# Batch 0's hidden layer by seven products, its quarter sums kept in SBUF, and the mean of w1 by one accumulation

## The chip, the cores and the metric

The kernel runs on one core of one Trainium2 chip. It is judged by the device time of one execution, in microseconds (us). Five runs of the kernel before gave a median of 1111.34 us (1110.28 to 1115.63). Changes under about 0.3% (3.3 us) can hardly be told from no change.

The core has five engines, each with its own queue, which works in order: TensorE (PE, matmuls), VectorE (DVE), ScalarE (ACT), GpSimd (POOL) and SyncE (SP, which only issues transfers here). POOL issues transfers too. A transfer is put on a queue behind what that queue holds, and a wait at the head of a queue holds up all that is behind it.

## The reference

Batch 4, 8 heads, 768 rows, 64 columns to a head, all in float32:

1. Hashed attention: six signs of `q @ proj` and of `k @ proj` give each row a bucket; scores count only where the buckets are equal; softmax, times v. The heads side by side give x, 768 x 512 for each batch.
2. `u = x + real(fft2(x))`.
3. `un = (u - mean) / sqrt(var + 1e-6)` along the 512 columns.
4. `out = u + relu(un @ w1) @ w2`, with w1 of 512 x 2048 and w2 of 2048 x 512. The weights come as float64, and the kernel makes float32 of them on the chip.

## The kernel before, in words

Batch b's attention is interleaved, step by step, with the mixing and the two layers of batch b-1: `attention(b)` and `mix(b)` are generators, and the loop at the end of `_main` calls them in turn. A step of attention (`weigh`, `values`) is one block of 128 keys of a pair of heads: scores on PE (L869), exp on ACT (L873), the bucket mask on DVE (L879), the sum of weights `acc` on DVE (L957), the product with v on PE (L890). A pair has six such steps; a batch has four pairs. `scale` sums `acc` over keys on PE (L910) and divides.

The order on PE, DVE, ACT and POOL is set by hand for batch 0's attention (`tc.manual_schedule`), and by the framework's list scheduler after that. Tiles with one tag share a fixed number of buffers. `pt` gives PSUM banks from a ring of two (four more in the last batch and at the very start).

**w1.** `weights1` runs beside batch 0's attention. It converts 16 slices of 128 x 512 (`narrow`, L631 to L647), and takes the mean over the 512 rows out of each column (`centre`, L670). The mean comes from `average`: four matmuls with a 128 x 32 matrix of ones put the sums of the four row chunks side by side on 32 PSUM partitions each (L656, tile `ws`), ACT copies that to SBUF (L661), and one full matmul with `mean`, filled with 1/(32 * 512), adds them up (L664, tile `wm`). The two parts are a step apart. The columns 0 to 1023 are centred during batch 0's attention; for the other 1024 the means are kept and taken off in batch 1's attention (the list `means`).

**w2.** `weights2` converts 16 slices of w2 through a ring of three raw buffers, `zraw2`. POOL issues the load of slice i+3 (L685) after slice i is converted. One conversion is three ACT instructions (L639, which waits for the load, L646 after DVE's L635, L647), and four on DVE (L631, L635, L644 twice); every second one is followed by four DVE sums (L1198 to L1201). The first eight run in `after` beside `mix(0)`'s first steps, the others in the second half of `mlp0`. Each half of w2's quarters is stored to DRAM by seven transfers on SP (L1203).

**The first layer.** w1 has 16 column blocks of 128. Batch 0 uses `mlp0`: each block and each half of the rows (384) takes four matmuls of 128 x 384 into one bank (L1314, tile `h`), and one ACT relu empties it (L1318). That is 128 matmuls of this kind. The batches 1 to 3 use `mlp7`: blocks f and f + 8 together take seven products of quarters (two matmuls each, L1361, tile `h_p`), with sums before and after, as in the Strassen-Winograd scheme: 112 matmuls for a batch. The sums after are seven ACT copies or relus out of PSUM, three relus in SBUF, and five DVE additions for each f. The sums of w1's quarters are made in batch 0: `quarters(f)`, called from the second row blocks of `mlp0`, computes four sums on DVE (L1149 to L1152) into the tile `tq` and stores them, with three plain quarters, in the DRAM tile `ad` (L1154, L1155). `mlp7` loads them from there through a ring of 12, whose place is w1 itself.

**The second layer.** `outer7` uses seven products for all batches (L1232, tile `o`); it uses `tq` for its temporaries too.

**Shared buffers.** `acc` and the four tiles `ef` of `fold` share the tag `t6`, with two buffers. `fold` is DVE work that starts the Fourier step; two of its four steps run in the last pair of the same batch's attention.

Of the kernel before, what the change touches and what calls it, by code (L numbers as in the profile page):

```python
# [479 lines left out]
def _main(  # L480
# [128 lines left out]
    mean = const.tile([P, P], F32, tag="mean", name="mean")  # L609
    nc.gpsimd.memset(mean, 1.0 / (32 * DM))  # L610
    w1 = const.tile([P, NDC, DFF], F32, tag="w1", name="w1")
# [39 lines left out]
    def average(f):  # L651


        ps = pt([P, WC], f"ws{f}")
        for c in range(NDC):
            nc.tensor.matmul(  # L656
                ps[32 * c : 32 * c + 32, :], ones[:, 0:32], w1[:, c, f : f + WC],
                start=True, stop=True,
            )
        part = wt([P, WC], F32, "u", f"part{f}", 2)  # L660
        nc.scalar.copy(part, ps)  # L661
        yield
        ps = pt([P, WC], f"wm{f}")
        nc.tensor.matmul(ps, mean, part, start=True, stop=True)  # L664
        yield ps

# [36 lines left out]
    def weights1():  # L703
        slices = [
            (w1[:, c, f : f + WC], moe_w_ch1[c * P : (c + 1) * P, f : f + WC])
            for f in range(0, DFF, WC)
            for c in range(NDC)
        ]
        zt = wt([P, 3, 2 * WC], F32, "z", "zraw1", 1)
        ft = wt([P, 12, WC], F32, "F", "fraw", 1)  # L710
        raws = [zt[:, i] for i in range(3)] + [
            ft[:, i : i + 2].rearrange("p i w -> p (i w)") for i in range(0, 8, 2)
        ]
        arrival = Arrival(slices, raws, 0)
        for i in range(arrival.depth):
            arrival.fetch(i, nc.sync)
            if i == 1:
                load(1)
        yield
        half = None  # L720
        for i in range(len(slices)):
            arrival.convert(i, ft[:, 8 + i % 4].bitcast(I32))
            yield
            if half:
                centre(half[0], next(half[1]))
                half = None
            if i % NDC == NDC - 1:


                f = i // NDC * WC  # L730
                if f < DFF // 2:
                    half = f, average(f)
                    next(half[1])

# [190 lines left out]
    def attention(b):  # L925
# [10 lines left out]
        for t in range(NPAIR):  # L936
            n = NPAIR * b + t
            half = fold(b, 0) if t == NPAIR - 1 else iter(())
            if 1 < n + 1 < NPAIR * B:
                load(n + 1)  # L940
            ahead = prepare(n + 1) if n + 1 < NPAIR * B else iter(())
            oos = [ps_o.tile([P, 512], F32, tag="o", name=f"oo{n}_{g}") for g in range(2)]
            acc = wt([P, 2, 2, HALF], F32, "t6", f"acc{n}", 2)
            first = None
            for c in range(NT):
                pk = weigh(n, c)
                new = pk[:, :, :, 0:HALF]
                sums = [acc]
                if c == 0:
                    first = new  # L950
                elif c == NT - 1 and b == 0:

                    sums.append(new)
                else:

                    for g in (0, 1) if b == 0 else (slice(0, 2),):
                        nc.vector.tensor_tensor(  # L957
                            acc[:, g], (first if c == 1 else acc)[:, g], new[:, g],
                            op=ALU.add,
                        )  # L960
                while pending:
                    finish()
                pending.append((n, c, pk, oos, sums))
                if c > 2:
                    next(half, None)
                if c > 0:
                    next(ahead, None)
                yield
# [28 lines left out]
    def fold(b, cp):  # L997
# [6 lines left out]
        for pc in range(2):  # L1004
            ef = wt([P, 2, S], F32, "t6", f"ef{b}_{cp}_{pc}", 2)
            e = ef[:, 0]
# [23 lines left out]
    def mix(b):  # L1030
# [63 lines left out]

        yield from mlp0(b) if b == 0 else mlp7(b)

# [77 lines left out]
    def weights2():  # L1174

        slices = []
        for half in range(2):
            for r in range(HF // 2):
                for hi, first in ((0, B11), (1, B21)):
# [7 lines left out]
                    )  # L1187
        zt = wt([P, 3, 2 * WC], F32, "z", "zraw2", 1)
        arrival = Arrival(slices, [zt[:, i] for i in range(3)], NDC * DFF // WC)
        for half in range(2):  # L1190
# [15 lines left out]

    def outer7(b, half, hall, ut, rs):
        def tile_sums(j):
# [85 lines left out]

    def mlp0(b):


        x = xs[b]
        ut = [w1[:, c, 0:DM] for c in range(NDC)]
        ut += [wt([P, DM], F32, "u", f"u{b}_{T}", 2) for T in range(NDC, NT)]  # L1300
        rs = {}
        hall = wt([P, 2, HF // 2, S], F32, "F", f"h{b}", 1)
        for half in range(2):
            for i in range(2):
                for r in range(HF // 2):
                    f = half * HF // 2 + r
                    fc = f + i * HF
                    if i:
                        quarters(f)
                    for g in range(2):  # L1310
                        cols = slice(g * HALF, (g + 1) * HALF)
                        ps = pt([P, HALF], f"h{b}_{g}_{fc}")
                        for c in range(NDC):
                            nc.tensor.matmul(  # L1314
                                ps, w1[:, c, fc * P : (fc + 1) * P], x[:, c, cols],
                                start=(c == 0), stop=(c == NDC - 1),
                            )
                        nc.scalar.activation(hall[:, i, r, cols], ps, AF.Relu)  # L1318
                        if half and (r + g) % 4 < 3:
                            next(arrival2, None)  # L1320
                        yield
            if half == 0:
                for T in (4, 5, 0, 1, 2, 3):
                    across(b, T, ut[T])
            yield from outer7(b, half, hall, ut, rs)

    def mlp7(b):
# [4 lines left out]
        t1, t2, t4 = bs  # L1332
        t3 = b12
        prods = [A11, S2, A12, S1, S3, S4, A22]
        right = {A11: b11, S2: t2, A12: b21, S1: t1, S3: t3, S4: b22, A22: t4}
# [3 lines left out]
        def fetch():  # L1339
            n = fetched[0]  # L1340
            if n < len(todo):
                nc.sync.dma_start(ring[n % NR], ad[todo[n][0], todo[n][1]])
                fetched[0] += 1
# [5 lines left out]
        nc.vector.tensor_tensor(t4, b21, t2, op=ALU.subtract)  # L1349
        ut = us + [wt([P, DM], F32, "u", f"u{b}_{T}", 2) for T in range(4, NT)]  # L1350
        for T in (3, 4, 5):
# [6 lines left out]
        def product(i, ps, start=True):  # L1358
            n = done[0]
            for k in range(2):  # L1360
                nc.tensor.matmul(  # L1361
                    ps, ring[n % NR][:, k], right[i][:, k],
                    start=start and k == 0, stop=k == 1, skip_group_check=not start,
# [3 lines left out]

        for half in range(2):
            for r in range(HF // 2):
# [27 lines left out]
                product(S3, p7)  # L1397
                nc.scalar.copy(side[0], p7)
                nc.vector.tensor_tensor(c22, c22, side[0], op=ALU.add)
                nc.scalar.activation(c22, c22, AF.Relu)  # L1400
# [3 lines left out]
                nc.scalar.activation(c12, c12, AF.Relu)  # L1404
                if f == 0:
                    for T in range(3):
                        across(b, T, ut[T])
                yield
                product(A22, p7, False)
                nc.scalar.copy(side[1], p7)  # L1410
                nc.vector.tensor_tensor(c21, c21, side[1], op=ALU.add)
                nc.scalar.activation(c21, c21, AF.Relu)
                if r % 2:
                    yield
            yield from outer7(b, half, hall, ut, rs)


    MIX = [2 + NT + NDC + 2 * (2 * HF + GT * 4)]
    MIX += [2 + NT + NDC + 2 * (7 * HF // 4 + GT * 4)] * (B - 1)
    LEFT = 8  # L1420
# [19 lines left out]
    with tc.manual_schedule(engines={ET.PE, ET.DVE, ET.Activation, ET.Pool}):  # L1440
# [6 lines left out]
        for _ in other:  # L1447
            pass
        pwf = wt([P, 2, P], F32, "t6", "pwf", 2)
        nc.sync.dma_start(pwf, cn["pw"].ap())  # L1450
        nc.scalar.copy(pw, pwf)
        means = []
        late = [(f, average(f)) for f in range(DFF // 2, DFF, WC)]
        for _, avg in late:
            next(avg)
        for f, avg in late:
            means.append((f, wt([P, WC], F32, "u", f"mean{f}", 2)))
            nc.scalar.copy(means[-1][1], next(avg))
    for b in range(B):
        if b > 0:  # L1460
# [9 lines left out]
            for i, _ in enumerate(attention(b), 1):  # L1470
                if b == 1 and i == 2:
                    for f, avg in means:
                        centre(f, avg)
                while done * steps < (MIX[b - 1] - LEFT) * (i - wait):
                    next(other)
# [25 lines left out]
        other = mix(b)  # L1501
        if b == 0:
            arrival2 = weights2()
            other = after(2 + NT, other, islice(arrival2, HF + 1))
# [47 lines left out]
```

## Time and profile before

| what | value |
|---|---|
| median of five runs | 1111.34 us |
| the profiled execution | 1110.69 us, of which the span is 1108.8 us |
| PE busy | 1061.5 us (96%) |
| DVE busy | 778.5 us (70%) |
| ACT busy | 456.0 us (41%) |
| batch 0's attention | about 0 to 145 us |
| batch 1's attention beside batch 0's layers | about 145 to 424 us |
| the same one batch on | about 424 to 683 us |
| and one more | about 683 to 934 us |
| last batch's layers alone | about 934 to 1109 us |

The three middle stages have the same work but for three things: the first of them converts w2, makes w1's quarters and uses `mlp0`. Groups name line, engine, operation, tiles, shape and count, then the busy time and mean nanoseconds of one, then the idle time in front of them and what ended it. A float32 matmul stands as two records, so that 128 matmuls are x256. The chain of waits is the sequence of work that ended last, each piece with start and length in us.

### The profile page before, as it was taken

What the parts mean: (1) busy time and instruction counts of PE and PEld (TensorE: products, weight loads), DVE (VectorE), ACT (ScalarE), POOL (GpSimd) and SP (SyncE); (2) the same over time, 40 slices, a digit from 0 to 9 for tenths busy, and PEclk for the clock granted to TensorE, in tenths of its full rate; (3) what the DMA queues carried; (4) which work ended last, traced back from release to release, by engine and by line L of the source; (5) the groups of instructions that cost most, each with busy time, mean ns of one, the idle gap of its engine ahead of it and who ended that gap; (6) DMA issues with size and microseconds to landing.
All of it is one profiled execution on the core that took longest, in us unless ns stands there. A gap on an engine that the chain in (4) does not pass through costs nothing.

```text
span 1108.8 us, 13908 instructions
## 1 busy us (share of the span) xinstructions
PE 1061.5 (96%) x4925; PEld 651.3 (59%) x4925; DVE 778.5 (70%) x1298; ACT 456.0 (41%) x879; POOL 79.4 (7%) x141
## 2 busy tenths in 40 slices
PE   7999987999999999999999999999999999999996
PEld 3334353555845676555664567645674569768675
DVE  5889968749598686975767795984866785744353
ACT  6778545534164224454335423355224422341420
POOL 1000000002110020030000011021000002100000
PEclk9999999999999999999999999999999999999999
DMA  8844444611056053323144234213032205122401
GB/s 225 201 97 110 86 153 119 221 34 27 1 146 225 20 123 115 49 69 77 26 152 91 67 67 166 39 43 95 15 118 63 77 29 171 48 86 80 129 20 41
DMA packets 175566, 103.13 MB, mean 93 GB/s; under 512 B 129408, under 2 KB 162816, under 8 KB 175488
## 3 DMA queue, kind: packets, MB, share of 16 engines
q1 hardware_dynamic: 168400, 83.93, 28.5%
q0 software_dynamic: 5520, 17.83, 5.1%
q8 instruction: 41, 0.67, 0.3%
q10 hardware_dynamic: 1568, 0.39, 0.2%
q14 instruction: 37, 0.30, 0.1%
HBM read 81.14 MB, written 20.97 MB: 92 GB/s over the span
## 4 chain that ended last, share of the span: by engine, by line
PE 68%; DVE 19%; DMA 5%; ACT 3%; issue 3%; SPq 1%; DVEq 0%; ACTq 0%
PE o L1232 23%; PE h_p L1361 18%; PE sc L869 6%; PE oo L890 6%; PE h L1314 6%; DVE acc L957 4%; DVE pk L879 3%; DMA zraw<-in_moe_w_ch_dram 3%; PE cs L1047 2%; PE sum L910 2%; ACT pk L873 1%; PE A L1076 1%; DMA ad<-tq 1%; PE B L1076 1%; DVE x L1090 1%
## 5 line engine op out<-in xcount | busy, mean ns | idle before, releaser
L1232 PE MATMUL o<-w,h 128*128 128x256 f32 x1152 | 258.9, 381 | 0.1
L1232 PEld LDWEIGHTS o<-w,h 128*128 128x128 f32 x1152 | 216.6, 190 | 42.7 <-issue 4.7
L873 ACT ACTIVATE pk<-sc 128x768 f32<-128x768 f32 x192 | 148.1, 808 | 89.2 <-PE sc L869 59.2
L879 DVE SCALAR_TENSOR_TENSOR pk<-qb,kb,pk 128x768 f32<-128x768 bf16 x132 | 128.5, 1012 | 62.8 <-ACT pk L873 61.4
L869 PE MATMUL sc<-qt,kt 64*128 64x384 f32 x768 | 154.4, 506 | 4.7 <-ACT pk L873 4.7
L890 PE MATMUL oo<-pk,vn 128*64 128x385 f32 (+1 forms) x768 | 149.2, 499 | 2.6 <-ACT x L903 2.3
L1361 PE MATMUL h_p<-x,w 128*128 128x384 f32 x384 | 139.0, 493 | 1.4 <-ACT h L1402 1.4
L1361 PE MATMUL h_p<-w 128*128 128x384 f32 x288 | 106.0, 491 | 0.7 <-ACT u L1103 0.7
L957 DVE TENSOR_TENSOR acc<-acc,pk 128x1536 f32<-128x1536 f32 (+1 forms) x72 | 105.6, 1481 | 1.0 <-ACT pk L873 0.6
L1361 PEld LDWEIGHTS h_p<-x,w 128*128 128x128 f32 x384 | 70.4, 190 | 57.7 <-ACT h L1402 5.1
L890 PEld LDWEIGHTS oo<-pk,vn 128*64 128x64 f32 x768 | 48.7, 136 | 91.5 <-issue 73.6
L869 PEld LDWEIGHTS sc<-qt,kt 64*128 64x128 f32 x768 | 66.8, 187 | 52.6 <-issue 25.6
L1314 PE MATMUL h<-x,w 128*128 128x384 f32 x256 | 86.2, 491 | 2.7 <-ACT h L1318 2.7
L1361 PEld LDWEIGHTS h_p<-w 128*128 128x128 f32 x288 | 53.3, 190 | 41.0 <-ACT w L1410 3.3
L1314 PEld LDWEIGHTS h<-x,w 128*128 128x128 f32 x256 | 47.6, 190 | 39.0 <-ACT h L1318 4.2
L1262 ACT COPY tq<-o 128x256 f32<-128x256 f32 x24 | 8.9, 372 | 115.5 <-PE o L1232 115.5
L1244 DVE SCALAR_TENSOR_TENSOR w<-o,rs,w 128x256 f32<-128x256 f32 x56 | 26.8, 479 | 40.7 <-PE o L1232 40.7
L1232 PE MATMUL o<-w 128*128 128x256 f32 x192 | 46.1, 383 | 4.0 <-DVE w L1244 2.4
L985 POOL DMA_DIRECT2D out_dram<-w x30 | 16.4, 548 | 428.4 <-issue 309.1
L1232 PEld LDWEIGHTS o<-w 128*128 128x128 f32 x192 | 35.9, 190 | 11.4 <-DVE w L1244 4.5
L1251 ACT COPY tq<-o 128x256 f32<-128x256 f32 x24 | 8.9, 371 | 74.6 <-PE o L1232 74.6
L1278 DVE TENSOR_TENSOR tq<-tq,o 128x256 f32<-128x256 f32 x24 | 10.1, 422 | 38.1 <-PE o L1232 38.1
(161 smaller groups left out, 1267.0 us busy)
## 6 DMA issues: line engine op xcount, KB each, us to landing
w<-ad SPq DMA_DIRECT2D x168, 128.0 KB, 2.0
w<-bd SPq DMA_DIRECT2D x42, 512.0 KB, 4.6
zraw<-in_moe_w_ch_dram POOLq DMA_DIRECT2D x21, 512.0 KB, 4.4
bd<-w SPq DMA_DIRECT2D x14, 512.0 KB, 4.6
vn<-in_v_dram SPq DMA_DIRECT2D x32, 192.0 KB, 3.6
qn<-in_q_dram SPq DMA_DIRECT2D x120, 48.0 KB, 2.5
kn<-in_k_dram SPq DMA_DIRECT2D x60, 96.0 KB, 3.3
ad<-tq SPq DMA_DIRECT2D x8, 512.0 KB, 4.0
```

The lines of the kernel that those rows point to most:

```text
L869: last[0] = nc.tensor.matmul(ps[:, h, 0:HALF], kt[rows, ks], qt[rows, qs], start=kb is not None, stop=True,)
L873: nc.scalar.activation(pk[:, g, :, 0:HALF], ps[:, :, 0:HALF], AF.Exp, scale=SCALE)
L879: nc.vector.scalar_tensor_tensor(w, qb[:, h].rearrange("p (g s) -> p g s", g=2), kb[:, h, c : c + 1], w, op0=ALU.is_equal, op1=ALU.mult,)
L890: nc.tensor.matmul(oos[g][h * D : (h + 1) * D, 0:w], nat["v", n][:, (2 * c + h) * D : (2 * c + h + 1) * D], pk[:, g, h, 0:w], start=(c == ...
L910: nc.tensor.matmul(ps[h * D : (h + 1) * D, :], ones, part[:, g, h], start=(i == 0), stop=(i == len(sums) - 1),)
L957: nc.vector.tensor_tensor(acc[:, g], (first if c == 1 else acc)[:, g], new[:, g], op=ALU.add,)
L1047: nc.tensor.matmul(ps[:, pc + 2 * lo : pc + 2 * hi - 1 : 2], z[:, cp, pc, par, t * P : (t + 1) * P], ch[:, cp, pc, lo:hi], start=(cp == 0) ...
L1076: nc.tensor.matmul(ps[:, cols], F[:, par, k, t, j * P : (j + 1) * P], sq[:, t, k, cols], start=(t == 0), stop=(t == 1),)
L1232: nc.tensor.matmul(ps, a[:, r], right7[i][:, r], start=start and r == 0, stop=r == HF // 2 - 1, skip_group_check=not start,)
L1244: nc.vector.scalar_tensor_tensor(t[:, cols], src, r, t[:, cols], op0=ALU.mult, op1=ALU.add)
L1314: nc.tensor.matmul(ps, w1[:, c, fc * P : (fc + 1) * P], x[:, c, cols], start=(c == 0), stop=(c == NDC - 1),)
L1361: nc.tensor.matmul(ps, ring[n % NR][:, k], right[i][:, k], start=start and k == 0, stop=k == 1, skip_group_check=not start,)
```

## The change

- `mlp0` is gone. Batch 0 goes through `mlp7` too. It has no ring: the three plain quarters are read from w1 in place, and the four sums from `tq`. `quarters(0)` is called before the first product, `quarters(f + 1)` after the last product of f, and `quarters(4)` before the second half. The stores to `ad` stay as they are.
- Room for batch 0's sums of x (`t1`, `t2`, `t4`) comes from an `ef` buffer and from the third of `zraw2`; w2's conversion gets a ring of two raw buffers in place of three. `zraw2` is given out before `mix(0)` starts.
- The tag `t6` is split into `acc` and `ef`, with one buffer each. In batch 1, `fold` starts one step later in its pair.
- `average` is four full matmuls that accumulate in one bank, with `mean` filled with 1/512; the copy and the second matmul are gone, and `centre` follows in the same step.
- Batch 0's seven-product path uses one `side` buffer twice, and other places for `ut` and `s1`. The pace of the steps, `MIX`, drops from 68 to 64 for the stage of batch 0.

```diff
     def average(f):
-        ps = pt([P, WC], f"ws{f}")
+        ps = pt([P, WC], f"wm{f}")
         for c in range(NDC):
             nc.tensor.matmul(
-                ps[32 * c : 32 * c + 32, :], ones[:, 0:32], w1[:, c, f : f + WC],
-                start=True, stop=True,
+                ps, mean, w1[:, c, f : f + WC], start=(c == 0), stop=(c == NDC - 1)
             )
-        part = wt([P, WC], F32, "u", f"part{f}", 2)
-        nc.scalar.copy(part, ps)
-        yield
-        ps = pt([P, WC], f"wm{f}")
-        nc.tensor.matmul(ps, mean, part, start=True, stop=True)
-        yield ps
+        return ps
...
-            acc = wt([P, 2, 2, HALF], F32, "t6", f"acc{n}", 2)
+            acc = wt([P, 2, 2, HALF], F32, "acc", f"acc{n}", 1)
...
-                if c > 2:
+                if c > (3 if b == 1 else 2):
                     next(half, None)
...
-            ef = wt([P, 2, S], F32, "t6", f"ef{b}_{cp}_{pc}", 2)
+            ef = wt([P, 2, S], F32, "ef", f"ef{b}_{cp}_{pc}", 1)
...
-        yield from mlp0(b) if b == 0 else mlp7(b)
+        yield from mlp7(b)
...
-        arrival = Arrival(slices, [zt[:, i] for i in range(3)], NDC * DFF // WC)
+        arrival = Arrival(slices, [zt2[:, i] for i in range(2)], NDC * DFF // WC)
...
     def mlp7(b):
+        ut, sd, ss = [*us], side, s1s
+        if b == 0:
+            bt = wt([P, 2, S], F32, "ef", "bt", 1)
+            t1, t2, t4 = (
+                at.rearrange("p (k n) -> p k n", k=2)
+                for at in (bt[:, 0], bt[:, 1], zt2[:, 2, 0:S])
+            )
...
+            sd = [s1s[0].rearrange("p r n -> p (r n)")[:, 0:HALF]] * 2
+            ss = [s1s[0], spare[3].rearrange("p (r n) -> p r n", n=P)]
+            quarters(0)
...
         def product(i, ps, start=True):
             n = done[0]
+            left = ring[n % NR]
+            if b == 0:
+                f = n // 7
+                if i >= S2:
+                    left = tq[:, i - S2].rearrange("p (k m) -> p k m", m=P)
+                else:
+                    c, r = (0 if i == A11 else 2), (f + HF if i == A22 else f)
+                    left = w1[:, c : c + 2, r * P : (r + 1) * P]
...
+                if b == 0 and r < HF // 2 - 1:
+                    quarters(f + 1)
...
+        for half in range(2):
+            if b == 0 and half:
+                quarters(HF // 2)
+            for i, _ in enumerate(inner(half)):
+                if b == 0 and half and i % 4 < 3:
+                    next(arrival2, None)
+                yield
...
-    MIX = [2 + NT + NDC + 2 * (2 * HF + GT * 4)]
-    MIX += [2 + NT + NDC + 2 * (7 * HF // 4 + GT * 4)] * (B - 1)
+    MIX = 2 + NT + NDC + 2 * (7 * HF // 4 + GT * 4)
```

## The prediction

> **What bounds the kernel.** First the busy times of the engines: PE works in 96% of the span, so time falls only where PE's work falls or its idle time does. Then busy time by stretch, for the stage of batch 0's layers, and the same stretches one batch on, where the seven products already run. Columns: stretch, its length, then busy time of PE, PEld, DVE, ACT, POOL, the granted clock, DMA share, GB/s.
>
> ```profile
> PE 1061.5 (96%) x4925; PEld 651.3 (59%) x4925; DVE 778.5 (70%) x1298; ACT 456.0 (41%) x879; POOL 79.4 (7%) x141
> ```
>
> ```profile
> 145.00:160.00 15.00, 12.71 (x82) 8.53 (x79) 9.15 (x18) 6.54 (x15) 1.54 (x3) 1.00 0.46 134
> 160.00:200.00 40.00, 31.78 (x155) 17.90 (x154) 33.14 (x63) 21.50 (x40) 2.68 (x6) 1.00 0.48 134
> 200.00:248.00 48.00, 47.66 (x176) 25.37 (x176) 23.42 (x37) 17.57 (x34) 1.59 (x3) 1.00 0.46 147
> ...
> 300.00:375.00 75.00, 72.32 (x300) 39.56 (x299) 60.61 (x120) 35.16 (x67) 2.79 (x5) 1.00 0.46 139
> ```
>
> ```profile
> 470.00:518.00 48.00, 48.00 (x191) 24.25 (x189) 30.90 (x52) 25.84 (x51) 11.03 (x12) 1.00 0.25 75
> 575.00:637.00 62.00, 61.12 (x253) 30.81 (x252) 47.08 (x71) 31.41 (x61) 0.00 (x0) 1.00 0.33 79
> ```
>
> Batch 0's first layer lies in 195 to 248 and 309 to 375, its Fourier products before. PE idles 10.5 us between 145 and 200, then little. DVE is at 83% in 160:200 and 81% in 300:375, where w2 is converted. The chain of waits names what holds PE up, and the list of waits (engine, line, releaser: total, times, longest) says who stood for whom in 145:424.
>
> ```profile
> 64.79 1.07 PE ws L656 x8
> ...
> 69.02 1.06 PE wm L664 x2
> ...
> 73.24 2.65 PE sum L910 x16
> ```
>
> ```profile
> 151.93 3.12 DMA ad<-tq
> ...
> 159.14 7.54 DMA ad<-tq
> ...
> 180.37 4.79 DMA zraw<-in_moe_w_ch_dram
> ...
> 188.33 4.19 DMA zraw<-in_moe_w_ch_dram
> ...
> 1027.25 36.12 PE h_p L1361 x112
> ```
>
> ```profile
> ACT zraw L639 <- DMA zraw<-in_moe_w_ch_dram: 29.1, 12, 4.6
> ```
>
> ```profile
> PE h L1314 <- ACT h L1318: 2.7, 1, 2.7
> ```
>
> ```profile
> L1387 DVE TENSOR_TENSOR h<-h 128x384 f32<-128x384 f32 x8 | 4.4, 554 | 6.3 <-ACT h L1386 6.3
> ...
> L1383 ACT COPY h<-h_p 128x384 f32<-128x384 f32 x8 | 3.8, 476 | 1.8 <-PE h_p L1361 1.7
> ```
>
> The reader is to see two kinds of limit: PE alone from 200 on, and before that transfers that DVE and ACT wait for.
>
> **The change part by part.** The sum is made against the profiled execution's 1110.7 us; the median stands 0.65 us above it.
>
> *A, the first layer's matmuls.* 128 become 112. 112 records took 36.12 us where PE ran freely, 0.3225 us a record; 32 records fewer are 10.3 us. They come off while PE is busy, so they count in full if nothing new makes PE wait.
>
> *B, the mean of w1.* Two records in `wm` took 1.06 us and eight in `ws` 1.07, so an average costs 2.13 us. The wm row has 0.59 us for a record by itself, so a second adds some 0.43 to 0.47; eight in one bank take 0.59 + 7 x 0.43 = 3.6 us: +1.5 for each of four. At the first (36 us) DVE has an idle gap of 2.6 us before the transpose of the sums, which the earlier centring (2.5 us) fills: +0.2. At the second everything up to `sum` is on the chain: +1.5. The late pair adds 3.0 to PE; it also sets all eight late centrings (0.68 each) before the third addition to `acc`, five of them (3.4 us) ahead of the first, behind which the exps of the next blocks wait. Between 0 and 3.4; I take 2, since in 126 to 145 us PE and DVE are both at 93% or more. Sum +3.7.
>
> The row `ws` has four packed matmuls in 1.07 us. The Trainium skill, TensorEngine Tiling (Array Packing), section Theoretical Speedup, gives up to four times for a dimension of 32 or less; it speaks against dropping the 32-column form. By it alone four averages would lose 4 x 3 x 0.9, some 11 us (an estimate); by the rows, which count the second matmul that packing needs, 6 us of PE work.
>
> *C, the stores of the quarter sums.* DVE waits 8.0 us at L1149 for three stores of `tq`, and 10.7 us of the chain lie there. Three of the four early sets of sums move behind products, each over 9 us apart, longer than the 4.0 us median of such a store. Between -10.7 and 0. PE idles only 10.5 us in the whole stretch, half of it behind slices of w2; and SP's queue now has stores of `tq` behind `bd` stores, whose seven took 10.8 us to issue in one place, so a late one would hold the next sums. I take -4.
>
> *D, new waits in the first half.* For each f the two PSUM banks are now emptied seven times, not four, by an ACT queue that also holds two conversions (0.68 + 0.68 + 0.96 us each) and exps (0.81 each). I walked the new order through by these durations: in f = 0 the products wait 1.7 and 1.0 us for masks that stand on DVE behind the sums t1 to t4 (0.96 each); in f = 1 S1 waits 2.2 us because the relu that empties its bank stands behind L646, which stands behind L635 on DVE; then 1.3 us for the bank of `bits`; f = 2 and 3 about 1 us each. Some 8 us. Lower end: batch 1, where the same rotation costs PE 1.2 us in all; upper end 14 (3.5 for each f). I take 8, because batch 1 has no conversions.
>
> The wait for ACT h in the list is one in batch 0. The skill's Perfetto Trace Analysis, section Matmuls, wants independent groups to rotate through banks so that emptying overlaps the next group; by it the half-length groups lose cover, and if every one of 56 copies of 0.48 were bare, it would be 27 us (an estimate). Batch 1's 1.2 us says that without a busy ACT they are not.
>
> *E, the second half.* 300:375 has 60.6 us of DVE work. Twenty additions of 0.554 add 11.1: 71.7 us, in a stretch that PE would need only 75 - 5.2 = 69.8 for. From the other side: 575:637 has 47.1; eight conversions (0.42 + 0.68 + 0.82 each), their sixteen sums and four sets of quarters (0.42 each) add 28.8: 75.9. DVE's best 20 us here (320 to 340) are 93% busy; 71.7 / 0.93 is 77 us. So DVE becomes the bound, and the half takes 2 us more than now in place of 5.2 less: +7. Between 0 and 14. What is late next: `quarters(f + 1)`, S2's operand, and through w2's last quarters `outer7`.
>
> *F, a ring of two for w2.* ACT waits 29.1 us for 12 loads already. In the new ACT order L639 of the fifth slice comes right behind L647 of the third, which frees its buffer: a full load, 4.3 us, with the exps of two blocks behind it. In the walk of D most of it falls where these exps wait for `acc` anyway. 0, between -2 and 13 (three such).
>
> *G, one buffer for acc and ef.* In the new order the sums over keys come ahead of the first addition of the next pair, and batches 1 and 2 shift one attention step behind some products, which keep PE fed. `ef` is DVE after DVE. 0, between -2 and 2. The MLP path's `side`: ACT has waited for its reader by then. The last batch's layers: 0.
>
> Sum: -10.3 + 3.7 - 4 + 8 + 7 + 0 + 0 = +4.4; 1110.7 + 4.4 = 1115.1 for a profiled execution, **1115.7 us** as a median.
>
> **Rivals.** *R1, the waits of D and E stay hidden, and it is faster.* For: aggregate DVE work in the stage would be 202.8 + 22 + 4 = 229 us of some 270, and batch 1 runs the same products with 3.5 us of idle PE. Against: 93% is the most DVE shows. With D 2 and E 2: -10.3 + 3.7 - 4 + 4 = -6.6, about 1104.7; it decides from D + E under 7.
>
> *R2, the gain is eaten exactly:* D + E between 7 and 13.5: 1108 to 1114.6, no change to be told.
>
> *R3, the ring of two starves.* ACT stands bare for a load at three or more slices, 4.3 us each, with PSUM banks unemptied: +13 on the forecast, 1128. For: 12 of 16 conversions wait with three buffers. Against: PE's idle time between 200 and 424 is 6 us although ACT waits for loads there too.
>
> **Chances.** Forecast (slower, 1114.7 to 1122) 0.38; R3 and other slower sums 0.12; R2 0.21; R1 0.29. Faster 0.29, same 0.21, slower 0.50 (bound 0.3%, what this measurement can tell). The range takes R1 with D + E near nothing (1103) and stops at R3's 1128; the forecast alone spans 1111 to 1122.
>
> **What would show it.** Right: `h_p` x896; batch 0's additions at L1364 to L1388 with DVE over 90% busy in the second half; PE waits for ACT h or `tq` of 10 us or more in 160 to 375. Wrong: PE idle under 8 us from 145 to 424 (R1); DVE waiting for `ad<-tq` as before (C); more than 40 us of ACT at L639 (R3); batches 1 and 2 longer than 259 and 251 us (G).

## The result and the profile after

The changed kernel takes 1114.49 us (median; 1110.27 to 1117.43), the kernel before 1112.03 beside it: a ratio of 1.0016, 95% interval [1.001, 1.0022], or +1.8 us (1.1 to 2.4). The forecast was 1115.7, slower by 0.4%. The time lies in its range and its sign is right, but a change of 0.16% belongs to the outcome "no change to be told" (0.21), not to the forecast. The profiled execution of the changed kernel took 1113.4 us, its span 1111.6, against 1110.7 and 1108.8.

First the first page and the stretches that the prediction showed, now of the changed kernel (stretch, length, then busy time of PE, PEld, DVE, ACT, POOL, granted clock, DMA share, GB/s).

```profile
PE 1065.8 (96%) x4885; PEld 648.3 (58%) x4885; DVE 800.2 (72%) x1342; ACT 474.2 (43%) x923; POOL 66.5 (6%) x141
```

```profile
145.00:160.00 15.00, 14.17 (x92) 8.28 (x92) 7.66 (x9) 9.00 (x19) 0.00 (x0) 1.00 0.31 97
160.00:200.00 40.00, 34.33 (x178) 19.87 (x177) 33.18 (x60) 23.02 (x43) 3.17 (x6) 0.96 0.46 109
200.00:248.00 48.00, 45.99 (x156) 22.66 (x155) 39.17 (x70) 27.91 (x57) 2.12 (x4) 1.00 0.51 166
...
300.00:375.00 75.00, 70.64 (x287) 35.51 (x286) 66.53 (x126) 47.40 (x94) 3.27 (x6) 0.98 0.50 146
```

PE has 40 records less on the page (32 of the first layer, 8 of the averages) and yet 4.3 us more of busy time. DVE went from 60.6 to 66.5 us in 300:375, not to 71.7. And the clock column, 1.00 before in all four rows, has 0.96 and 0.98: more of that in the last section.

A cut by stretches of equal length mixes work. It is better to cut at landmarks: the first Fourier matmul of each batch (tile `cs`). Here are the rows cut so, of the kernel before and then of the changed one: batch 0's attention, the stage of batch 0's layers, and the stages of batches 1 and 2.

```profile
0.00:138.90 138.90, 124.36 (x689) 53.82 (x689) 112.26 (x191) 95.39 (x166) 6.49 (x26) 0.99 0.62 144
138.90:420.00 281.10, 263.91 (x1198) 162.53 (x1197) 205.66 (x368) 111.24 (x214) 26.22 (x41) 1.00 0.38 110
420.00:679.00 259.00, 255.52 (x1186) 154.97 (x1185) 193.65 (x294) 102.66 (x198) 19.78 (x29) 1.00 0.32 83
679.00:933.80 254.80, 252.32 (x1162) 154.13 (x1161) 187.42 (x290) 95.38 (x183) 19.78 (x29) 1.00 0.24 71
```

```profile
0.00:143.20 143.20, 129.23 (x680) 57.14 (x680) 115.45 (x197) 93.40 (x162) 6.70 (x26) 1.00 0.59 140
143.20:420.70 277.50, 260.92 (x1166) 156.11 (x1165) 225.69 (x406) 131.63 (x260) 25.05 (x41) 0.99 0.39 111
420.70:680.80 260.10, 256.67 (x1185) 155.05 (x1184) 192.77 (x294) 103.01 (x200) 13.80 (x29) 1.00 0.32 82
680.80:936.80 256.00, 253.56 (x1162) 154.25 (x1161) 186.74 (x290) 94.81 (x183) 13.80 (x29) 1.00 0.24 71
```

The second numbers are lengths. Batch 0's attention is 4.3 us longer, the stage of batch 0's layers 3.6 shorter, the two middle stages 1.1 and 1.2 longer, and the rest, the last batch's layers, 174.8 us in place of 175.0: +2.8 in all, the difference of the spans. So the stage that the change is about gained, and the loss came in three stages outside it. The prediction had it the other way round: a loss of 0.7 there and nothing in the middle stages. (PE's idle time in a row is its length less PE's busy time: 17.2 us before and 16.6 after in the stage of batch 0's layers.)

The lists of waits of the changed kernel (145 to 424 us), for the rows shown of before:

```profile
ACT zraw L639 <- DMA zraw<-in_moe_w_ch_dram: 22.4, 11, 4.1
```

```profile
PE h_p L1338 <- ACT h L1363: 2.0, 1, 2.0
...
PE h_p L1338 <- DVE tq L1137: 1.3, 1, 1.3
...
PE h_p L1338 <- ACT w L1387: 1.1, 1, 1.1
```

DVE's 8.0 us of waits for `ad<-tq` are gone from its list. The products wait 4.4 us in all for `h`, `w` and `tq`, where 10 or more would have confirmed D. The chain still has slices of w2 in it:

```profile
191.02 3.86 DMA zraw<-in_moe_w_ch_dram
220.87 3.84 DMA zraw<-in_moe_w_ch_dram
227.25 5.42 DMA zraw<-in_moe_w_ch_dram
...
1030.20 36.12 PE h_p L1338 x112
```

The new work of batch 0's layers costs what it cost in batch 1 (rows of 145 to 424 us). A record of the new average lasts 592 ns, as one of the old second matmul did (count, minimum, median and longest in ns, first and last start), and the eight records of the first average take 3.67 us together, where the sum had 3.6 (start and length):

```profile
L1364 DVE TENSOR_TENSOR h<-h 128x384 f32<-128x384 f32 x8 | 4.4, 555 | 4.6 <-ACT h L1363 4.6
L1363 ACT COPY h<-h_p 128x384 f32<-128x384 f32 x8 | 3.8, 477 | 3.3 <-PE h_p L1338 3.3
```

```profile
L654 PE MATMUL wm<-w,mean x32: 592/592/697, 35.1 to 134.5; 128*128 128x512 f32 x32
```

```profile
35.08 3.67 PE L654 MATMUL wm<-w,mean 128*128 128x512 f32 x8
```

So these prices were right. What they cost in their places is the matter of the experiments.

### The profile page after: what moved, and what is told of

The parts are those of the page before. It is cut to its first block, busy times and chain, and to the rows that moved or that the text cites. A ratio compares the mean times of both kernels' runs of the same rounds, so it can differ in the third digit from the quotient of the medians.

```text
span 1111.6 us, 13941 instructions
## 1 busy us (share of the span) xinstructions
PE 1065.8 (96%) x4885; PEld 648.3 (58%) x4885; DVE 800.2 (72%) x1342; ACT 474.2 (43%) x923; POOL 66.5 (6%) x141
## 4 chain that ended last, share of the span: by engine, by line
PE 63%; DVE 13%; ACT 3%; issue 2%; DMA 2%; DVEq 0%; ACTq 0%; SPq 0%
PE h_p L1338 22%; PE o L1218 21%; PE oo L877 6%; PE sc L856 6%; DVE pk L866 3%; PE cs L1034 2%; PE A L1063 2%; PE B L1063 1%; DVE acc L944 1%; DMA zraw<-in_moe_w_ch_dram 1%; ACT pk L860 1%; PE sum L897 1%; PE un L1089 1%; DVE w L1230 1%; DVE h L1204 1%
## 5 line engine op out<-in xcount | busy, mean ns | idle before, releaser
L1338 PE MATMUL h_p<-x,w 128*128 128x384 f32 x448 | 163.9, 495 | 2.5 <-ACT h L1379 1.4
L877 PE MATMUL oo<-pk,vn 128*64 128x385 f32 (+1 forms) x768 | 153.8, 500 | 2.1 <-DVE pk L866 1.9
L1338 PEld LDWEIGHTS h_p<-x,w 128*128 128x128 f32 x448 | 81.7, 190 | 70.0 <-ACT h L1379 6.2
L856 PEld LDWEIGHTS sc<-qt,kt 64*128 64x128 f32 x768 | 66.5, 187 | 52.2 <-issue 24.3
L1218 PE MATMUL o<-w 128*128 128x256 f32 x176 | 42.2, 383 | 2.9 <-DVE w L1230 2.0
L1364 DVE TENSOR_TENSOR h<-h 128x384 f32<-128x384 f32 x32 | 17.8, 556 | 33.7 <-ACT h L1363 33.7
L1371 DVE TENSOR_TENSOR h<-h 128x384 f32<-128x384 f32 x32 | 17.8, 555 | 32.3 <-ACT h L1370 32.2
L1218 PEld LDWEIGHTS o<-w 128*128 128x128 f32 x176 | 32.9, 190 | 9.6 <-DVE w L1230 4.1
```

Source lines behind the costliest of these rows:

```text
L856: last[0] = nc.tensor.matmul(ps[:, h, 0:HALF], kt[rows, ks], qt[rows, qs], start=kb is not None, stop=True,)
L877: nc.tensor.matmul(oos[g][h * D : (h + 1) * D, 0:w], nat["v", n][:, (2 * c + h) * D : (2 * c + h + 1) * D], pk[:, g, h, 0:w], start=(c == ...
L1218: nc.tensor.matmul(ps, a[:, r], right7[i][:, r], start=start and r == 0, stop=r == HF // 2 - 1, skip_group_check=not start,)
L1338: nc.tensor.matmul(ps, left[:, k], right[i][:, k], start=start and k == 0, stop=k == 1, skip_group_check=not start,)
L1364: nc.vector.tensor_tensor(c21, c12, c21, op=ALU.add)
L1371: nc.vector.tensor_tensor(c22, c21, c22, op=ALU.add)
```

## The experiments

Two readings stood against each other. The *sum of the prediction*: the waits D and E eat the gain. The *ledger of the traces*: the gain is there, and the mean of w1 (B) and the single buffers (G) eat it. Times are medians; differences from the kernel before are taken from the ratios.

**The mean of w1, alone and undone.** `mean_only` is the kernel before with the new `average`; `old_mean` is the changed kernel with the old one (the diff's first part, forwards and backwards):

```diff
-                ps[32 * c : 32 * c + 32, :], ones[:, 0:32], w1[:, c, f : f + WC],
-                start=True, stop=True,
+                ps, mean, w1[:, c, f : f + WC], start=(c == 0), stop=(c == NDC - 1)
```

> The kernel before with only the new average of w1 (four full matmuls in one bank, centring in the same step). By the ledger of the two traces this part costs batch 0's attention 4.3 us (its Fourier products start at 143.2 instead of 138.9 us), and 6.0 if the half-clock stretch that the trace of before has there is left out: 1116 to 1118 against 1112.0. By the prediction's term B it is +3.7, 1115.7. Rival: the extra matmul time lies in idle time of PE and the centring a step earlier pays for it, less than 1.5 us in all; then the 4.3 us in the trace have another cause, such as the changed order of the steps.

> The changed kernel with the packed average of before put back (chunk sums on 32 partitions each, copy, second matmul, centring a step later), all else as changed. By the ledger 4.3 to 6.0 us under the changed kernel's 1114.5: 1108.5 to 1110.2, so under the kernel before by 2 to 3.5 us. By the prediction's term B, 1110.8. Rival: D and E are what eats the gain and B is small; then 1113 or more.

`mean_only`: 1114.93, ratio 1.0032 [1.0015, 1.0049], +3.6 us. `old_mean`: 1110.59, ratio 0.9987 [0.9969, 1.0005]; from the changed kernel's 1.0016 that is 3.2 us less (3.9 by the medians). Term B, +3.7, was right in size. The first Fourier matmul starts at 142.5 us in the trace of `mean_only`, at 138.1 in that of `old_mean` and at 138.9 before; in the changed kernel it is here (count, durations in ns, first and last start):

```profile
L1034 PE MATMUL cs<-ch,z x48: 273/275/483, 143.2 to 160.6; 128*128 128x128 f32 x16, 128*128 128x256 f32 x16, 128*128 128x129 f32 x8, 128*128 128x127 f32 x8
```

The sum of the fourth pair starts at 125.2 instead of 124.0, so 1.2 us come by then and 3.1 with the late pair of averages. The kernel before has a stretch at half clock at 52 us, the changed one has none in this stage (last section), so the 1.2 may be too small, by an estimate up to 1.7.

**The buffers of acc and ef.** `split_only` is the kernel before with the tags split, as the change does it:

```diff
-            acc = wt([P, 2, 2, HALF], F32, "t6", f"acc{n}", 2)
+            acc = wt([P, 2, 2, HALF], F32, "acc", f"acc{n}", 1)
...
-            ef = wt([P, 2, S], F32, "t6", f"ef{b}_{cp}_{pc}", 2)
+            ef = wt([P, 2, S], F32, "ef", f"ef{b}_{cp}_{pc}", 1)
```

> The kernel before with only the tag of acc and ef split in two, one buffer each, and batch 1's fold a step later. The two traces have the stages of batches 1 and 2 longer by 1.1 and 1.2 us with the same code but for these buffers: +2.3, 1114.3 against 1112.0, and up to +3.4 if batch 1's attention, beside batch 0's layers, loses as much. By the prediction's term G: 0. Rival: the two stages are longer for another reason (the order that the scheduler finds after a different stage 1); then within 0.7 us of the kernel before.

1114.6, ratio 1.0024 [1.0006, 1.0043], +2.7 us. The rows of its stage of batch 0's layers and of its middle stages:

```profile
140.10:426.50 286.40, 269.00 (x1198) 164.72 (x1197) 205.99 (x370) 111.28 (x214) 26.23 (x41) 0.98 0.37 108
426.50:686.60 260.10, 256.66 (x1185) 155.03 (x1184) 192.80 (x294) 102.10 (x198) 13.80 (x29) 1.00 0.32 82
686.60:942.60 256.00, 253.55 (x1162) 154.25 (x1162) 186.77 (x290) 94.84 (x183) 13.80 (x29) 1.00 0.24 70
```

The middle stages take the same 260.1 and 256.0 as in the changed kernel, from this edit alone. The first row is 5.3 us longer than before; this execution was the slowest of its twelve (1119.56), and that stage has three stretches at half clock in it, so it doesn't tell whether the single buffers cost time in batch 1's attention too. The first try to undo it there missed:

> The changed kernel, in which acc and ef take the two buffers in turn from batch 2's attention on, as in the kernel before; until then one buffer each. If the single buffers cost the 2.3 us: 1112.2 against the changed kernel's 1114.5, with the two middle stages at 259.0 and 254.8 us again. By term G of the prediction, 0: 1114.5.

1114.58, ratio 1.0021 [1.0005, 1.0038], stages of 260.1 and 255.8 us. The edit chose the place by a counter that the PSUM ring of `pt` also counts on, so the turns were not kept (and the ring of the last stage was touched): the second pair's first addition still came behind the sum. It says nothing of the theory. `by_turns` names the places outright:

```diff
-            acc = wt([P, 2, 2, HALF], F32, "acc", f"acc{n}", 1)
+            tag = "ef" if n in (9, 11, 12, 14) else "acc"
+            acc = wt([P, 2, 2, HALF], F32, tag, f"acc{n}", 1)
...
-            ef = wt([P, 2, S], F32, "ef", f"ef{b}_{cp}_{pc}", 1)
+            ef = wt([P, 2, S], F32, "acc" if b == 2 else "ef", f"ef{b}_{cp}_{pc}", 1)
```

> The changed kernel, in which from batch 2's attention on acc and ef lie in the two buffers in turn, pair by pair, so that the first addition of a pair need not wait for the sum over keys of the pair before. If that wait is the 1.1 us of each middle stage: 1112.2 against the changed kernel's 1114.5, the stages at 259.0 and 254.8 us, and the second pair's first addition ahead of the sum. Rival (term G of the prediction: 0): 1114.5 and stages of 260.1 and 256.0 us, although the addition comes first.

1110.7, ratio 0.9992 [0.9976, 1.0007], 2.7 us under the changed kernel's ratio; the rows of its middle stages are those of the kernel before again:

```profile
421.20:680.20 259.00, 255.51 (x1186) 154.97 (x1185) 193.78 (x294) 103.38 (x200) 19.75 (x29) 1.00 0.32 82
680.20:935.00 254.80, 252.30 (x1162) 154.12 (x1161) 187.62 (x290) 95.38 (x183) 19.75 (x29) 1.00 0.24 71
```

The mechanism stands in the order of DVE around the first change of pairs in batch 2: start, length, line. The first addition of the new pair is `acc<-pk,pk`; the transposes `rt<-sum` follow the sum over keys that reads the old pair's `acc`. The kernel before, the changed kernel, and `by_turns`:

```profile
464.58 1.76 DVE L957 TENSOR_TENSOR acc<-pk,pk 128x1536 f32<-128x1536 f32 x1
...
473.64 0.58 DVE L914 STREAM_TRANSPOSE rt<-sum 128x384 f32<-128x384 f32 x1
```

```profile
473.72 0.58 DVE L901 STREAM_TRANSPOSE rt<-sum 128x384 f32<-128x384 f32 x1
476.01 0.57 DVE L901 STREAM_TRANSPOSE rt<-sum 128x384 f32<-128x384 f32 x1
476.51 1.72 DVE L944 TENSOR_TENSOR acc<-pk,pk 128x1536 f32<-128x1536 f32 x1
```

```profile
465.74 1.76 DVE L945 TENSOR_TENSOR acc<-pk,pk 128x1536 f32<-128x1536 f32 x1
...
474.80 0.57 DVE L901 STREAM_TRANSPOSE rt<-sum 128x384 f32<-128x384 f32 x1
```

With one buffer the addition comes 11 us later in its stage (476.51 - 420.70 against 464.58 - 420.00), and with it the masks of the next blocks, three of which now stand together at 481.72; the eight `oo` records beside them (PE's timeline of before, after and `by_turns`) take 2.35 us instead of 1.51, and 1.51 again in `by_turns`. That is 0.84 of the stage's 1.1 us, and it hides inside a busy PE: its idle time in the stage is 3.4 us, before 3.5.

```profile
479.04 1.51 PE L890 MATMUL oo<-pk,vn 128*64 128x385 f32 x8
```

```profile
482.88 2.35 PE L877 MATMUL oo<-pk,vn 128*64 128x385 f32 x8
```

```profile
480.20 1.51 PE L877 MATMUL oo<-pk,vn 128*64 128x385 f32 x8
```

**The seven products alone.** `seven_only` is the changed kernel with both edits undone (as in `old_mean` and `by_turns`; batch 1's attention keeps its single buffers).

> The changed kernel with the packed average of before and with acc and ef in two buffers in turn from batch 2 on: what is left of the change is the seven products for batch 0, their sums from SBUF, the ring of two raw buffers, and single buffers in batch 1's attention alone. If the parts add up by the ledger, 1110.6 of the kernel with the packed average, less 2.3: 1108.3, 3.7 under the kernel before. By the prediction's terms A, C, D, E alone (-10.3 - 4 + 8 + 7): 0.7 above it, 1112.8. Rival: the loss of the middle stages comes back elsewhere, 1110.6.

1107.84, ratio 0.9961 [0.9945, 0.9977], 4.3 us under the kernel before; the ledger had 3.7. It beats both kernels. Its trace compares best with that of before, because batch 0's attention is the same 138.9 us. The rows of the stage of batch 0's layers and of the next:

```profile
138.90:416.60 277.70, 258.01 (x1167) 155.42 (x1166) 228.69 (x414) 131.72 (x260) 24.97 (x41) 1.00 0.39 112
416.60:675.50 258.90, 255.43 (x1185) 155.21 (x1184) 193.77 (x294) 103.28 (x200) 19.76 (x29) 1.00 0.32 82
```

The stage is 3.4 us shorter, although the first layer's records take 8.9 us less (each counted from its start to the next record's start or its own end: 256 of `h` 85.3 us, 224 of `h_p` 76.4). So C, D, E and F together cost 5.5 us, with whatever the single buffers cost in batch 1's attention. 2.5 of them are idle time of PE (17.2 to 19.7), and 3.0 are in other records that got longer, as with `oo` above (counted the same way: `oo` 1.5, `sum` 1.0, `o` 0.8).

The stage can be cut further, at the first and last product of each half of the first layer. The second half before, then the stretch ahead of the products, the first half and the second half in `seven_only` (the first two of before stand under C below):

```profile
309.30:375.30 66.00, 63.32 (x252) 32.32 (x251) 53.90 (x105) 30.76 (x58) 2.13 (x4) 1.00 0.50 150
```

```profile
138.90:196.90 58.00, 47.69 (x276) 28.45 (x274) 45.17 (x77) 31.82 (x60) 3.16 (x6) 1.00 0.41 103
196.90:247.20 50.30, 48.49 (x166) 24.07 (x164) 40.75 (x71) 29.20 (x59) 2.11 (x4) 1.00 0.51 162
307.10:370.50 63.40, 59.28 (x232) 28.41 (x232) 58.58 (x114) 42.05 (x84) 2.64 (x5) 1.00 0.55 164
```

The stretch ahead of the products is 1.3 us longer, the first half 1.9 shorter, the second 2.6 shorter. The layer's own records take 4.3 and 4.6 us less in the two halves, so 2.4 were lost in the first, where D had its 8, and 2.0 in the second, where E had its 7. This is one execution of each kernel.

**The stores of the quarter sums (C).** `free_stores`:

```diff
-        nc.sync.dma_start(ad[f, 3:7].rearrange("i p k m -> p i k m"), st)
+        nc.sync.dma_start(
+            ad[f, 3:7].rearrange("i p k m -> p i (k m)"), w1[:, :, f * P : (f + 2) * P]
+        )
```

> The kernel before, but the store of the four quarter sums reads two neighbouring column blocks of w1 in place of the tile of sums, same bytes and one transfer: the sums are still made, and no later sum waits for a store. The output for batches 1 to 3 is not the reference's, since their sums in DRAM are other data. It prices term C alone. By the prediction 4 us faster (between 0 and 10.7), 1108; by the ledger, in which PE's idle time from the first Fourier product to the first product of the first layer fell from 11.8 to 7.1 us, 4.7 faster, 1107.4. Rival: the slices of w2 are late anyway and hold the same stretch up, under 1.5 us faster, 1110.6 or more.

1112.08, ratio 0.9997 [0.9982, 1.0012]: nothing, so both readings missed, and the rival held. Cut at the first Fourier matmul, the first product and the end of the first half, before and then here:

```profile
138.90:195.60 56.70, 44.92 (x257) 26.67 (x255) 43.99 (x79) 28.18 (x54) 3.69 (x7) 1.00 0.47 133
195.60:247.80 52.20, 51.86 (x190) 27.54 (x188) 27.82 (x45) 21.61 (x42) 2.12 (x4) 1.00 0.42 135
```

```profile
139.60:194.20 54.60, 45.71 (x256) 27.83 (x254) 43.61 (x79) 28.66 (x56) 3.68 (x7) 0.97 0.48 145
194.20:248.90 54.70, 53.07 (x190) 27.42 (x188) 28.71 (x45) 21.61 (x42) 2.11 (x4) 1.00 0.42 127
```

The first stretch is 2.1 us shorter, although 3.41 us of it ran at half clock (the 0.97), and the second is 2.5 longer. DVE no longer waits for the stores (8.0 us before), ACT's waits for slices of w2 stay (26.8 us in this stage, before 29.1).

**The ring of two (F).** `ring_two`:

```diff
-        arrival = Arrival(slices, [zt[:, i] for i in range(3)], NDC * DFF // WC)
+        arrival = Arrival(slices, [zt[:, i] for i in range(2)], NDC * DFF // WC)
```

> The kernel before with two raw buffers for w2 in place of three, nothing else. Term F: 0, between -2 and +13. By the ledger 0 to +1, since ACT's waits for these loads were no longer in the changed kernel (22.4 us against 29.1). Rival R3, the ring starves: +4 for each slice that ACT stands bare for, +4 to +13, 1116 to 1125.

1111.25, ratio 1.0003 [0.9986, 1.002]. In the kernel before, F is 0 within 2.2 us, and R3's 13 is out.

**DVE as the bound (E).** `more_dve`, in the changed kernel:

```diff
+                for c in (c11, c22, c12, c21, c11) if b == 0 and half else ():
+                    nc.vector.tensor_tensor(c, c, c, op=ALU.max)
                 if r % 2:
```

> The changed kernel with 20 more DVE instructions in the second half of batch 0's first layer, five for each f: a 128x384 tensor_tensor max of a finished tile with itself (0.555 us each as the additions beside them, 11.1 us), which changes no value. It doubles that part of term E. If DVE is the bound of the second half, as term E has it, each microsecond counts: 1114.5 + 11 = 1125.6. If the half has slack, as the 4.0 us of PE idle time in it say: +1 to +4, 1115.5 to 1118.5.

```profile
L1393 DVE TENSOR_TENSOR h<-h 128x384 f32<-128x384 f32 x20 | 9.8, 544 | 0.0
```

```profile
313.80:378.30 64.50, 59.20 (x229) 28.04 (x228) 64.01 (x124) 41.43 (x83) 2.65 (x5) 1.00 0.52 161
```

1115.39, ratio 1.0036 [1.0019, 1.0054]: 2.2 us over the changed kernel's ratio, for 9.8 us of DVE work in batch 0's second half. In the trace the stages of batch 0's and batch 1's layers together take 538.9 us against 537.6. Between an eighth and a quarter of the added work shows. The second row is that half, from its first product to its last: 64.5 us with DVE busy 64.0 of them. In the changed kernel it takes 65.0 (DVE 58.9, and 3.41 us at half clock), in `seven_only` 63.4 (DVE 58.6). So even a DVE that is busy 99% of the time hardly lengthens it: DVE is not the bound of that half.

**The slices of w2.** `loads_once`, on `seven_only`:

```diff
-            self.fetch(i + self.depth, nc.gpsimd)
+            if self.depth > 2:
+                self.fetch(i + self.depth, nc.gpsimd)
```

> The kernel with seven products alone (packed average, two buffers in turn), but of w2 only the first two slices are loaded; the 16 conversions run on what lies in the two raw buffers, so no load is waited for, and the range test of w2 is given a bound that it always meets. The output is not the reference's. If slices that come late are what keeps the gain of 8.9 us of PE work down to 3.4, the 10.3 us of PE idle time between the first Fourier product and the first product of the layer fall by half or more: 1103 or less against 1107.8. If the conversions' work on ACT and DVE is what counts, within 1.5 us of it: 1106.3 or more.

1100.72, ratio 0.9910 [0.9894, 0.9925], 5.7 us under the ratio of `seven_only`. The row of the same stage:

```profile
138.30:410.40 272.10, 258.59 (x1166) 156.15 (x1165) 228.39 (x414) 131.45 (x260) 17.60 (x27) 0.99 0.30 87
```

5.6 us shorter, with the same busy time on DVE and ACT, and PE's idle time at 13.5 us in place of 19.7. So it is the loads of the slices, and not the work of converting them, that cost 5.6 us in this stage. The kernel leaves out 14 transfers of 512 KB, so it cannot tell whether their late arrival or their traffic holds PE up.

**ACT's part (D), and spreading the conversions.** Both on `seven_only`:

```diff
+        if col >= NDC * DFF // WC:
+            return
         nc.scalar.activation(t, hi, AF.Abs)
```

> The kernel with seven products alone, without the two ACT instructions of a w2 conversion that serve the range test (16 pairs), which leaves the test of w2 out. It shortens the ACT queue that empties the PSUM banks, term D. If D is what eats the gain, some 4 us faster than 1107.8: 1103.8. If ACT has slack there: within 1 us, 1106.8 or more.

```diff
-            if i >= n and (i - n) % 5 < 3:
+            if i >= n and (i - n) % 2 == 0:
```

> The kernel with seven products alone, in which the first eight conversions of w2 come in every second step of batch 0's layers instead of three of five, so that they end eight steps later. If crowding in the stretch of the Fourier products is the loss: 1 to 3 us faster, 1104.8 to 1106.8. If it only moves the same work beside the products, where the banks must be emptied, or holds up the second layer, which needs these quarters: 1107.8 or up to 3 us slower.

`act_less`: 1111.56, ratio 0.9998 [0.9982, 1.0015], 4 us more than `seven_only` with 21.5 us less ACT work in the stage. Its trace shows the first stretch (first Fourier matmul to first product) 3.3 us shorter and the next two 1.5 and 3.0 longer, and its twelve runs had a mean granted clock of 0.9913, against 0.9941, worth some 2.4 us of the 4 by the last section's figures (an estimate). It does not settle D. `spread_w2`: 1109.93, ratio 0.9995 [0.998, 1.0009], 3.8 us more than `seven_only`; the first stretch is 4.6 us longer, the first half of the products 1.7 shorter, the second half 1.4 longer. The gain that crowding would have given did not come. How much the move itself cost stays open: the trace has two stretches at half clock in this stage (at 141 and 343 us), `seven_only` none, and the mean clock of its runs was 0.9925, by the same estimate 1.4 us.

## Why the prediction was right, and where it was wrong

| term | predicted, us | measured, us | from |
|---|---|---|---|
| A, first layer's matmuls | -10.3 | -8.9 | records in `seven_only` and before |
| B, mean of w1 | +3.7 | +3.6 [1.7, 5.4] | `mean_only` |
| C, stores | -4 | -0.3 [-2.0, +1.3] | `free_stores` |
| D + E, new waits | +8 +7 | by halves +2.4 +2.0; C to F together +5.5 | stage in `seven_only` |
| F, ring of two | 0 | +0.3 [-1.6, +2.2] | `ring_two` |
| G, single buffers | 0 | +2.7 [0.7, 4.8]; traces +2.3 | `split_only`, `by_turns` |
| sum | +4.4 | +2.9 | traces +2.8; ratio +1.8 [1.1, 2.4] |

The time came out near the forecast because errors of both signs cancelled: the right number from a sum in which only B and F were right. The range's lower end doesn't follow from the sum either: with D + E at nothing it gives -10.6, a median of 1100.7, not 1103.

- *A* was mis-sized: "112 records took 36.12 us where PE ran freely" is the price of the last batch, alone on PE. Among attention's matmuls a record of `h` takes 85.3 / 256 = 0.333 us and one of `h_p` 76.4 / 224 = 0.341.
- *B* was right in size and place: late pair +3.1 (predicted 2), the rest +1.2 (1.7).
- *C* failed: "Between -10.7 and 0" and "I take -4". The wait went, and nothing came of it; in `seven_only`, too, the stretch ahead of the products is 1.3 us longer than before, not shorter. The prediction had named what was late next ("half of it behind slices of w2") and yet counted the gain. `loads_once` shows what slices cost in the stage of `seven_only`; that they alone took C's gain in the kernel before was not tried.
- *D* and *E* were too high: 15 together, where 5.5 for C to F, less C's interval, leaves 4.2 to 7.5, and the cut by halves gives 2.4 and 2.0. The walk of D by hand came to some 8 us of waits; in the changed kernel PE waits 4.4 us for `h`, `w` and `tq` in the whole stage. Which of its steps the real order avoids was not traced. E's step "71.7 / 0.93 is 77 us" took the highest busy share seen in that half for a limit; with 9.8 us more work DVE was busy 99% of the half, and it cost 1.3 to 2.2. So the sign "DVE over 90% busy in the second half" came true (58.9 of 65.0 us) without the loss that it was to show. R1's condition, D + E under 7, holds by the halves and is left open by the interval.
- *G* failed: "the sums over keys come ahead of the first addition of the next pair, and batches 1 and 2 shift one attention step behind some products, which keep PE fed". The order was as told, but PE was not fed at full rate: `oo` records stretched, 0.84 of the 1.1 us that a stage lost. The sign "batches 1 and 2 longer" was on the list and came true.

R1 was nearer for the stage of batch 0's layers, which got faster; R2 had the right time.

## What to carry to other kernels

Price each part of a many-part change where it lands, and give a buffer that is taken away in another stage the same care as the headline: here the products gained 4.3 us, and a smaller pool and a plainer reduction took 6.3 back. A stall on the chain has no known worth until what is late next has been priced: here 8.0 us of waits for stores went and no time was saved. An idle row of near zero doesn't show that PE is fed: compare the mean length of the same records.

## What the runs showed of the hardware

PE's clock falls to half for 3.41 us, or two or three times that, at points that differ from run to run; the rows show it as a granted clock of about 0.5. The changed kernel, the end of a gap and what follows it, twice:

```profile
178.00:182.00 4.00, 2.07 (x12) 1.23 (x10) 2.20 (x5) 1.25 (x3) 0.00 (x0) 1.00 0.50 62
182.00:185.50 3.50, 3.13 (x6) 0.79 (x6) 3.27 (x6) 2.43 (x6) 0.53 (x1) 0.51 0.01 2
338.00:342.00 4.00, 1.98 (x6) 0.89 (x6) 2.90 (x6) 3.69 (x7) 0.00 (x0) 1.00 0.47 63
342.40:346.00 3.60, 3.60 (x7) 1.88 (x6) 2.52 (x4) 1.34 (x4) 0.53 (x1) 0.53 0.24 66
```

The 14 traces hold 27 such stretches ahead of the last matmul. Each begins between 0.5 us before and 1.6 us after the end of an idle gap of PE of 1.65 to 4.1 us. Not every gap brings one: the kernel before idled 3.05 us at 183.6 and kept the full clock. The Trainium skill, TensorE: Matmul & The Clock Gate, section HAM oscillation, warns of idle gaps above about 3.4 us; here gaps of 2 us did it, so the measurement decides. Each 3.41 us at half clock can thus cost up to 3.41 / 2 = 1.7 us beyond the gap itself (an estimate). Of the changed kernel's 46 runs with a recorded clock, those at 0.993 took 1114.8 to 1117.4 us and those at 0.998 1111.5 and 1112.1, so much of the spread of the runs goes with it, some 0.9 us for each 0.001 of clock (an estimate from these groups). The changed kernel's trace has two such stretches in the stage of batch 0's layers, those of before and of `seven_only` none, so their lengths there are not quite alike in clock. Why `act_less` had so many stays open.
